# Loading x in quarters and beginning attention on the first of them

## The chip, the cores and the metric

One Trainium2 chip, one of its cores. The metric is the time of the kernel on the device in microseconds (us), the median of several runs. The core has a matrix engine (TensorE, PE), a vector engine (VectorE, DVE), an engine for activation functions (ScalarE, ACT), a general one (GpSimd, POOL), and a queue engine that issues most of the transfers (SyncE, SP). Each works through its own list of instructions in order and waits on semaphores for the others.

## The reference

Two attention blocks over sequences of 2048 rows with 1024 features, 32 heads of 32 features each. Their outputs stand side by side in the result. All tensors are bf16.

```python
def A(x, wqkv, wo):                       # plain softmax attention
    q, k, v = split(x @ wqkv)             # 32 heads, 2048 x 32 each
    p = softmax(q @ k.T * 32 ** -0.5)     # over all 2048 keys, no mask
    return concat_heads(p @ v) @ wo

def B(x, wq, wk, wv, wo, beta):           # four segments of 512 rows, one after the other
    for s in range(4):
        a_dot = softmax(q_s @ k_s.T * scale + causal_mask) @ v_s
        a_mem = phi(q_s) @ M / (phi(q_s) @ z + 1e-6)
        o_s = sigmoid(beta) * a_mem + (1 - sigmoid(beta)) * a_dot
        M += phi(k_s).T @ v_s ; z += sum(phi(k_s))
    return concat(o) @ wo
```

Block A dominates: 32 heads of 2048 x 2048 scores, every one of which goes through an exponential.

## The kernel before

**Tiling.** The 32 heads of A are worked in eight groups of four (`g`, 0 to 7). A group's queries are cut into eight chunks of 256 (`c`). Scores are computed transposed, keys on the 128 partitions: a tile is 512 columns, two blocks of 128 keys (`kt`) by 256 queries of one head. Two or three such tiles make one exponential on ACT (`plan_op`, line 774), 128 x 1536 or 128 x 1024, from PSUM to a tile `P` in SBUF. PSUM has eight banks: two slots of three banks take the scores in turn (`SLOT_BANKS`), bank 6 (`X_BANKS`) serves all projections one after the other, bank 7 collects the attention output. Lines 823 and 829 multiply `P` with the values and with ones, for the output and for the softmax's denominator; `norm` divides (lines 847 to 898).

**Guard.** The exponential needs an upper bound of the scores as its bias, or it could overflow. It comes from the squared lengths of keys and queries: squares (`square_dve` or `square`), a product with `blk32` that sums them by head (`guard_cols`, line 989), a maximum over columns (line 996), a spreading of the results over partitions by a product with ones (`guard_end`, line 1016 and a product at line 450), another maximum (line 1026), and the bias column (line 1034).

**Order.** The work is listed with keys (`item`), and a scheduler in the Python program (`Prog.schedule`) lays it out once, by planned costs and due times, into one fixed list per engine. Exponentials follow the order of `units`; the projections of later groups, B's work and the output projections are `jobs` with an earliest and a latest time, spread by `level` and placed between score tiles by `pick`. The constants `STICK`, `OVER`, `MARGIN`, `LEAD_A`, `DUE_SLOPE`, `XR`, `OUT_D` steer that placement. What the program writes down is only the order; the engines then run as their semaphores allow.

**Beginning** (`plan_prologue`). ACT issues the loads of group 0's key and query weights (`W_A`). SP issues x of A, transposed on the way: eight transfers of 1024 rows x 128 features for the first half, then the value weights `Wv_A`, then eight for the second half (line 1052). PE multiplies the first half (`half0`): keys and queries 0 to 1023 of group 0, in banks 0 to 3. Then the first guard, in bias column 16 (`BIAS0`), and the value products (`job_VA`), of which three are evicted by ACT (line 1142).

**First half of the keys.** All of group 0's first four chunks run over the first half of the keys only (`part` 0: tiles 0 to 3), with that guard; their unnormalized results are parked in `OT_B`, which is still free (line 878). When the second half of keys and queries has been projected, the guard is renewed over all keys (`guard_A0`); the parked results are scaled by `f0`, the exponential of the difference of the two biases (line 1004), and added to the second half's (`part` 1, line 881). B's x (`xT_B`, line 950), its weights and beta (`graw`, line 1089) are loaded by SP behind A's x.

Of the kernel before, what the change touches and what calls it, by code (L numbers as in the profile page):

```python
# [5 lines left out]
dt = mybir.dt  # L6
# [4 lines left out]
P = 128  # L11
# [19 lines left out]
BIAS0 = 16  # L31
# [14 lines left out]
class Group:  # L46

    __slots__ = ("pe", "rd", "left", "free")

    def __init__(self):  # L50
        self.pe, self.rd = [], []
        self.left, self.free = 0, 0.0
# [82 lines left out]
STICK = 0  # L135
OVER = 0.1
# [3 lines left out]
MARGIN = 1.5  # L140
FILL = 0.0
RXJ = 4
LEAD_A, LEAD_B, DUE_AT, DUE_SLOPE = 12.0, 12.0, 8.0, 0.5
HOLD = {}
XR = 6
XC = 0
OUT_D = 60.0
# [3 lines left out]
class Prog:  # L151
# [39 lines left out]
    def schedule(self):  # L191
        pend = {}
        groups = list(dict.fromkeys(o.grp for o in self.ops if o.grp is not None))
        for g in groups:
            own = {*g.pe, *g.rd}
            first = g.pe[0]
            first.gate = [(x, 0.0) for o in g.pe[1:] for x in (o.deps | o.order) - own]
            first.gate += [(x, sum(o.dur for o in g.pe)) for o in g.rd for x in (o.deps | o.order) - own]
            g.left = len(g.rd)
            assert g.rd and not any(x.grp is g and x not in own for x in first.deps)  # L200
# [48 lines left out]
        def pick(t, av, c):  # L249
# [8 lines left out]
            best = None  # L258
            for x in av:
                if x.urgent:  # L260
                    continue
                if x.pvn is None and x.key > st["prog"] + AHEAD and not cold:
                    d = x.dur + (SWITCH if x.mode != mode else 0.0)
                    if x.key < st["prog"] + FILL and d <= slack + OVER:
                        v = (False, 1e3, x.key)
                        if best is None or v < best[0]:
                            best = (v, x)
                    continue
                d = x.dur + (SWITCH if x.mode != mode else 0.0)
# [9 lines left out]
                v = (d > slack + OVER, k, x.key)  # L279
# [138 lines left out]
class _Kernel:  # L418
# [74 lines left out]
    def alloc(self):  # L493
# [6 lines left out]
        self.r_xT = [[Res(), Res()] for _ in range(8)]  # L500
# [70 lines left out]
        self.f0 = sb("f0", [P, 1], dt.float32)  # L571
        self.r_f0 = Res()
# [5 lines left out]
        self.sm_xT = [[self.sem(f"d_xT{i}{h}") for h in range(2)] for i in range(8)]  # L578
# [13 lines left out]
    def plan(self):  # L592
# [14 lines left out]
        units = [("A", 0, c, p) for p in range(2) for c in range(4)] + [u + (None,) for u in units[4:]]  # L607
        tiles = [self.tiles_att_A(i, k, p) if kind == "A" else self.tiles_att_B(i, k) for kind, i, k, p in units]
        n = 0
        while n < len(units):  # L610
# [4 lines left out]
            if n == 0:  # L615
# [6 lines left out]
    def joins(self, a, b):  # L622

        return a[0] == b[0] == "A" and a[1] == b[1] and (a[3] == 0) == (b[3] == 0)
# [36 lines left out]
    def tiles_att_A(self, g, c, part=None):  # L661
# [3 lines left out]
        lo, hi = (0, 8) if part is None else (4 * part, 4 * part + 4)  # L665
        for t in range(lo, hi):
# [3 lines left out]
            for h in range(4):  # L670
                tiles.append(dict(unit=("A", g, c), kind="A", g=g, c=c, h=h, w=512, pieces=pieces, set=key, part=part, pv=pv,
                                  bias=BIAS0 if part == 0 else g % 2))
# [192 lines left out]
    def norm(self, t, key):  # L865
# [6 lines left out]
        if t["part"] is not None:  # L872
# [3 lines left out]
            if t["part"] == 0:  # L876
# [4 lines left out]
            self.dve(lambda e: e.scalar_tensor_tensor(out=st1, in0=st1, scalar=self.f0[:, 0:1], in1=src, op0=ALU.mult,  # L881
                                                      op1=ALU.add), 512, k, [ob, self.r_f0] + rs1, rs1)
# [3 lines left out]
        if kind == "A":  # L886
            T2, r2 = self.recip_rows(lsrc, ro, QC, k)
            q = QC * t["c"]
            if g >= 6 and self.r_xT[g][0].tag == ("dead",):
                rd = self.r_OTx[g - 6][t["c"]] = Res()  # L890
                self.pg.after(rd, self.r_xT[g][t["c"] // 4])
# [70 lines left out]
    def xbank(self):  # L962
        b = X_BANKS[0]
        self.bank[b] = Res(Group())
# [17 lines left out]
    def guard_cols(self, key, sqs, ncols):  # L982

        b = self.xbank()
# [15 lines left out]
    def guard_A0(self, key):  # L1000
        col = self.guard_cols(key, self.sqA[(0, 0)] + self.sqA[(0, 1)], 512)
        self.guard_end(key + 0.2, [self.col0, col], 2, [0], halves=True)
        rb, r0 = self.r_bias[0], self.r_bias[BIAS0]
        x = self.act(lambda e: e.activation(self.f0[:, :], self.bias[:, BIAS0:BIAS0 + 1], ACT.Exp, bias=self.bias[:, 0:1],
                                            scale=-1.0), 1, key + 1.0, [rb, r0], [self.r_f0])
# [5 lines left out]
    def guard_end(self, key, cols, nper, bias_cols, halves=False):  # L1011
# [6 lines left out]
        b = self.xbank()  # L1018
# [481 lines left out]
```

## Time and profile before

| | |
|---|---|
| three runs | 1207.85 us median, 1207.67 to 1208.72 |
| the profiled execution | 1211.64 us |
| its span, first to last instruction | 1209.8 us |
| ACT / PE / DVE / POOL busy | 1167.5 / 1128.0 / 557.7 / 216.6 us |
| DMA | 65.68 MB moved, 54 GB/s over the span |
| mean granted PE clock | 0.990 |

The profile is one execution on the chip. Its page gives busy time by engine, groups of instructions by line of the program with the mean duration of one (ns) and the idle time ahead of them with what ended it, and the chain of work that ended last. The trace behind it can be asked for a timeline of one engine (start, duration, engine, line, operation, tiles), for the rows of one tile, and for busy times in chosen stretches. In a timeline, `x15` means that 15 instructions of a kind followed one another and the duration covers all of them. Letters after an engine, as in SPq and ACTq, are its queue: the issuing of a transfer, which counts as time of the issuing engine and is not the transfer itself.

### The profile page before, as it was taken

What the parts mean: (1) busy time and instruction counts of PE and PEld (TensorE: products, weight loads), DVE (VectorE), ACT (ScalarE), POOL (GpSimd) and SP (SyncE); (2) the same over time, 40 slices, a digit from 0 to 9 for tenths busy, and PEclk for the clock granted to TensorE, in tenths of its full rate; (3) what the DMA queues carried; (4) which work ended last, traced back from release to release, by engine and by line L of the source; (5) the groups of instructions that cost most, each with busy time, mean ns of one, the idle gap of its engine ahead of it and who ended that gap; (6) DMA issues with size and microseconds to landing.
All of it is one profiled execution on the core that took longest, in us unless ns stands there. A gap on an engine that the chain in (4) does not pass through costs nothing.

```text
span 1209.8 us, 52848 instructions
## 1 busy us (share of the span) xinstructions
PE 1128.0 (93%) x24712; PEld 544.6 (45%) x24712; DVE 557.7 (46%) x1254; ACT 1167.5 (96%) x867; POOL 216.6 (18%) x279
## 2 busy tenths in 40 slices
PE   6999999999999999989999999999899999989997
PEld 4444434464444445534444444454444444433443
DVE  1243353443443545556453564565435555543224
ACT  3899999999999999999999999999999999998997
POOL 1121131311320211122210330312103221010000
PEclk9999999999999999999999999999999999998999
DMA  9812323202111312202301122102112410000101
GB/s 176 207 37 53 85 53 57 63 16 68 52 30 46 72 41 42 65 22 51 85 18 42 41 51 50 54 22 46 53 51 59 147 26 12 29 20 28 37 29 36
DMA packets 165675, 65.68 MB, mean 54 GB/s; under 512 B 135248, under 2 KB 162640, under 8 KB 165456
## 3 DMA queue, kind: packets, MB, share of 16 engines
q1 hardware_dynamic: 163088, 61.51, 20.8%
q8 instruction: 193, 3.16, 1.1%
q10 hardware_dynamic: 2368, 0.79, 0.3%
q14 instruction: 26, 0.21, 0.1%
HBM read 39.00 MB, written 11.73 MB: 42 GB/s over the span
## 4 chain that ended last, share of the span: by engine, by line
ACT 69%; PE 21%; DVE 5%; issue 3%; SPq 1%; DMA 1%; POOL 0%; DVEq 0%; ACTq 0%
ACT P L774 67%; PE ps L450 11%; PE ps L759 5%; PE ps L823 3%; PE ps L829 2%; ACT PKQ_B L1174 1%; SPq L1052 1%; DVE T L847 1%; DVE PKQ_B L1179 1%; DMA Wv_A<-in_A_wqkv_dram 1%; DVE KQ_B L973 0%; DVE T L856 0%; POOL P L786 0%; DVE OT_B L1200 0%; DVE KQ_A L973 0%
## 5 line engine op out<-in xcount | busy, mean ns | idle before, releaser
L774 ACT ACTIVATE P<-ps,bias 128x1536 bf16<-128x1536 f32 (+3 forms) x826 | 1149.1, 1664 | 16.2 <-PE ps L759 8.0
L829 PE MATMUL ps<-P,onesb 128*32 128x256 bf16 (+1 forms) x4864 | 300.1, 271 | 0.0
L759 PE MATMUL ps<-KQ_A 32*128 32x256 bf16 x4096 | 277.1, 275 | 19.3 <-ACT P L774 15.8
L823 PE MATMUL ps<-P,V_A 128*32 128x256 bf16 x4096 | 259.3, 276 | 8.5 <-ACT P L774 7.0
L759 PEld LDWEIGHTS ps<-KQ_A 32*128 32x128 bf16 x4096 | 80.6, 92 | 240.6 <-ACT P L774 130.7
L450 PE MATMUL ps<-xT_A,W_A 128*32 128x512 bf16 x2048 | 147.5, 390 | 11.4 <-DMA xT_A<-in_A_x_dram 6.5
L450 PE MATMUL ps<-xT_B,W_B 128*32 128x512 bf16 x2048 | 142.0, 381 | 4.4 <-DVE cols L996 1.4
L823 PEld LDWEIGHTS ps<-P,V_A 128*32 128x32 bf16 x4096 | 108.8, 96 | 79.0 <-issue 41.8
L829 PEld LDWEIGHTS ps<-P,onesb 128*32 128x32 bf16 x4864 | 130.7, 97 | 26.2
L786 POOL TENSOR_SCALAR_AFFINE_SELECT P<-P 128x768 bf16<-128x768 bf16 (+2 forms) x128 | 81.7, 662 | 254.9 <-ACT P L774 254.8
L979 POOL TENSOR_TENSOR sqB<-KQ_B 128x512 bf16<-128x512 bf16 x64 | 67.2, 1049 | 319.7 <-DVE KQ_B L973 274.9
L979 POOL TENSOR_TENSOR sqA<-KQ_A 128x512 bf16<-128x512 bf16 x60 | 63.1, 1051 | 293.5 <-DVE KQ_A L973 218.7
L973 DVE CAST KQ_B<-ps 128x512 bf16<-128x512 f32 x64 | 44.1, 690 | 123.6 <-PE ps L450 122.2
L1250 DVE CAST outsb<-ps 128x512 bf16<-128x512 f32 x56 | 38.7, 691 | 135.2 <-PE ps L450 134.1
L847 DVE STREAM_TRANSPOSE T<-ps 128x256 f32<-128x256 f32 (+1 forms) x148 | 72.5, 490 | 54.1 <-PE ps L829 39.8
L973 DVE CAST KQ_A<-ps 128x512 bf16<-128x512 f32 x60 | 41.5, 691 | 119.9 <-PE ps L450 116.1
L450 PE MATMUL ps<-Wv_A,xT_A 128*32 128x256 bf16 x2048 | 71.7, 274 | 6.6 <-issue 2.4
L856 DVE STREAM_TRANSPOSE T<-rc 128x256 f32<-128x256 f32 (+1 forms) x152 | 73.3, 485 | 4.0
L450 PEld LDWEIGHTS ps<-xT_A,W_A 128*32 128x32 bf16 x2048 | 45.7, 97 | 63.1 <-issue 31.7
L450 PE MATMUL ps<-Wv_B,xT_B 128*32 128x512 bf16 x1024 | 70.5, 382 | 2.4 <-DVE KQ_B L973 0.6
L450 PE MATMUL ps<-Wo_B,OT_B 128*32 128x512 bf16 x1024 | 70.8, 389 | 1.0 <-DVE KQ_B L973 0.6
L450 PEld LDWEIGHTS ps<-xT_B,W_B 128*32 128x32 bf16 x2048 | 45.6, 95 | 52.2 <-issue 25.5
(82 smaller groups left out, 754.4 us busy)
## 6 DMA issues: line engine op xcount, KB each, us to landing
Wv_B<-in_B_wv_dram SPq DMA_DIRECT2D x8, 1024.0 KB, 5.9
W_B<-in_B_wk_dram SPq DMA_DIRECT2D x32, 256.0 KB, 3.1
W_B<-in_B_wq_dram SPq DMA_DIRECT2D x32, 256.0 KB, 3.1
out_dram<-outsb SPq DMA_DIRECT2D x56, 128.0 KB, 1.9
W_A<-in_A_wqkv_dram SPq DMA_DIRECT2D x14, 256.0 KB, 3.2
ot_a_scratch<-OTst SPq DMA_DIRECT2D x51, 64.0 KB, 1.8
xT_A<-ot_a_scratch SPq DMA_DIRECT2D x6, 512.0 KB, 7.5
Wv_A<-in_A_wqkv_dram SPq DMA_DIRECT2D x4, 512.0 KB, 5.4
```

The costliest lines, as they stand in the source:

```text
L450: ins = e.matmul(out[r], w[:, r], x, start=start, stop=stop, tile_position=(0, 32 * t), skip_group_check=True)
L759: ins = e.matmul(out, kap, qap, start=st, stop=True, tile_position=(32 * h, 0), skip_group_check=True)
L774: a = self.act(lambda e: e.activation(dst, src, ACT.Exp, bias=self.bias[:, bc:bc + 1], scale=SCALE), cols, key, res + [self.r_bias[bc]], [rP])
L786: self.pool(lambda e, v=v, pat=pat: e.affine_select(v, v, pattern=pat, compare_op=ALU.is_ge, fill=0.0, base=0, channel_multiplier=-1), (m ...
L823: ins = e.matmul(self.ps[32 * h:32 * h + 32, 512 * obk + q0:512 * obk + q0 + nq], vt[:, c0 + 32 * h:c0 + 32 * h + 32], Pt[:, b, off:off + nq],
L829: ins = e.matmul(self.ps[32 * h:32 * h + 32, lcol + q0:lcol + q0 + nq], self.onesb[:, 0:32], Pt[:, b, off:off + nq], start=False, stop=las ...
L847: self.dve(lambda e: e.transpose(T1[:, 0:n], src), n, key, rsrc, [r1])
L856: self.dve(lambda e: e.transpose(T2[:, 0:n].rearrange("p (b r) -> p b r", r=32), bc), n, key, [rr], [r2])
L973: self.dve(lambda e: e.tensor_copy(dst, out), ncol, key + 1.0, [self.bank[b]], rdst)
L979: self.pool(lambda e: e.tensor_tensor(sq[:, :], src, src, ALU.mult), 512, key, [rsrc], [rs], rate=0.5)
L1052: self.dma(lambda e, i=i, h=h: e.dma_start(self.xT[:, i, 1024 * h:1024 * h + 1024], xa[1024 * h:1024 * h + 1024, P * i:P * i + P], transpo ...
L1250: self.dve(lambda e: e.tensor_copy(ob[:, :], self.ps[:, 512 * b:512 * b + 512]), 512, key + 1.0, [self.bank[b]], [ro])
```

## The change

x is loaded in quarters of 512 rows: 32 transposing transfers in place of 16, with `Wv_A` behind the first eight. `half0` becomes `quarter`, called for the first and the second quarter. Attention begins with chunks 0 and 1 over the first quarter of the keys (`part` 0, four exponentials of 1536 columns and two of 1024), goes on with chunks 0 and 1 over the second quarter and chunks 2 and 3 over the first half (`part` 1, sixteen exponentials), then with all over the second half (`part` 2). The guard is renewed twice: from bias column 17 to 16 after the second quarter, and from 16 to 0 after the fourth; the parked results are scaled by `fp[:, 0]` and `fp[:, 1]`. While x loads, PE multiplies zeros (`warm`, seven sets of four products of 512 columns). Of the value products only the first is evicted by ACT. Some planner constants have other values, and `pick` weighs the openings of bank 6 one at a time.

```diff
-BIAS0 = 16
+BIAS_PART = (17, 16)
+PARTS = ((0, 0), (0, 1), (1, 0), (1, 1), (1, 2), (1, 3), (2, 0), (2, 1), (2, 2), (2, 3))
+WARM = 7
...
-STICK = 0
-OVER = 0.1
+STICK = 0.5
+OVER = 0.3
...
-MARGIN = 1.5
-FILL = 0.0
+MARGIN = 0.5
...
-LEAD_A, LEAD_B, DUE_AT, DUE_SLOPE = 12.0, 12.0, 8.0, 0.5
+LEAD_A, LEAD_B, DUE_AT, DUE_SLOPE = 15.0, 12.0, 8.0, 0.3
-XR = 6
+XR = 0
-OUT_D = 60.0
+OUT_D = 90.0
...
-        units = [("A", 0, c, p) for p in range(2) for c in range(4)] + [u + (None,) for u in units[4:]]
+        units = [("A", 0, c, p) for p, c in PARTS] + [u + (None,) for u in units[4:]]
...
-        lo, hi = (0, 8) if part is None else (4 * part, 4 * part + 4)
+        lo, hi = {None: (0, 8), 0: (0, 2), 1: (2 if c < 2 else 0, 4), 2: (4, 8)}[part]
...
+    def guard_more(self, key, sqs, i, old, new):
+
+        ci, rc = self.guard_cols(key, sqs)
+        self.bank[X_BANKS[0]].grp.chain = True
+        c0, r0 = self.colrun
+        self.dve(lambda e: e.tensor_tensor(self.cols[:, ci:ci + 1], self.cols[:, ci:ci + 1], self.cols[:, c0:c0 + 1], ALU.max), 1,
+                 key + 0.1, [rc, r0], [rc])
+        self.colrun = (ci, rc)
+        self.guard_end(key + 0.2, [self.colrun], 2, [new], bank=X_BANKS[0])
+        x = self.act(lambda e: e.activation(self.fp[:, i:i + 1], self.bias[:, old:old + 1], ACT.Exp, bias=self.bias[:, new:new + 1],
+                                            scale=-1.0), 1, key + 1.0, [self.r_bias[old], self.r_bias[new]], [self.r_fp[i]])
+        x.margin = MARGIN
...
+        def warm(key):
+            self.dve(lambda e: e.memset(dummy[:, :], 0.0), 512, key, (), [rd])
+            for _ in range(WARM):
+                self.pe(lambda e: self.mm4(e, self.ps[:, 512 * 5:512 * 6], dummy[:, 0:P], dummy[:, :], True, True), 0.43, key, [rd],
+                        [self.bank[5]])
+        self.item(-99.5, warm)
...
-            for h in range(2):
+            for h in range(4):
                 for i in range(8):
                     mark([self.r_xT[i][h]], "x")
-                    self.dma(lambda e, i=i, h=h: e.dma_start(self.xT[:, i, 1024 * h:1024 * h + 1024],
-                                                             xa[1024 * h:1024 * h + 1024, P * i:P * i + P], transpose=True),
-                             self.sm_xT[i][h], key, [], [self.r_xT[i][h]], issue=1.55 + 0.1 * h, lat=3.2)
+                    self.dma(lambda e, i=i, h=h: e.dma_start(self.xT[:, i, 512 * h:512 * h + 512],
+                                                             xa[512 * h:512 * h + 512, P * i:P * i + P], transpose=True),
+                             self.sm_xT[i][h], key, [], [self.r_xT[i][h]], issue=0.68 if h < 2 else 0.85, lat=3.2)
...
+            if c == 0:
+                for x in self.r_KQA[0]:
+                    mark(x, "KQ", 0)
+                self.colrun = self.guard_cols(key, sq, bank=3)
+                self.guard_end(key, [self.colrun], 2, [BIAS_PART[0]], bank=4)
+            else:
+                self.guard_more(key, sq, 0, *BIAS_PART)
+        self.item(-50.0, lambda key: quarter(key, 0, (0, 1)))
+        self.item(-49.0, lambda key: self.job_VA(0, 0, key, 5, "ACT"))
+        self.item(-48.0, lambda key: quarter(key, 1, (6, 7)))
+        self.item(-47.0, lambda key: self.job_VA(0, 1, key, behind=True))
...
+        for c in (2, 3):
+            for kq in range(2):
+                add(8.0 * c - 9.0, p2 - 4.0, KQ, lambda key, kq=kq, c=c: self.job_KA(0, kq, c, key))
+        add(15.0, p2 - 4.0, 0.4, lambda key: self.guard_A0(key + 2.0))
```

## The prediction

> **What bounds the kernel now.** I read the page's busy shares first, then the ACT timeline for the gaps, then the beginning: SP's timeline, and the rows of the transposing loads by tile.
>
> ```profile
> PE 1128.0 (93%) x24712; PEld 544.6 (45%) x24712; DVE 557.7 (46%) x1254; ACT 1167.5 (96%) x867; POOL 216.6 (18%) x279
> L774 ACT ACTIVATE P<-ps,bias 128x1536 bf16<-128x1536 f32 (+3 forms) x826 | 1149.1, 1664 | 16.2 <-PE ps L759 8.0
> ```
>
> ScalarE (ACT) bounds it: 826 exponentials, 96% of the span. So the time is: start of the first exponential, plus the exponentials, plus ACT's gaps, plus the tail. The ACT timeline gives all four:
>
> ```profile
> 22.30 1.54 ACT L774 ACTIVATE P<-ps,bias 128x1536 bf16<-128x1536 f32 x1 [0.84 <-DVE bias L1034]
> 26.60 21.81 ACT L774 ACTIVATE P<-ps,bias 128x1536 bf16<-128x1536 f32 x15
> 50.23 5.41 ACT L774 ACTIVATE P<-ps,bias 128x1536 bf16<-128x1536 f32 x4 [1.82 <-PE ps L759]
> 58.41 2.97 ACT L774 ACTIVATE P<-ps,bias 128x1536 bf16<-128x1536 f32 x2 [1.48 <-DVE bias L1034]
> 64.87 101.94 ACT L774 ACTIVATE P<-ps,bias 128x1536 bf16<-128x1536 f32 x71
> 1166.39 35.63 ACT L774 ACTIVATE P<-ps,bias 128x1536 bf16<-128x1536 f32 x26 [1.05 <-PE ps L829]
> ```
>
> The first exponential (no. 1) starts at 22.30. A streaming one takes 21.81/15 = 1.454 us, one of 1024 columns about 1.05 (50.23 to 55.64 is three and one). No. 23, the first with the second guard, starts at 58.41, no. 26 at 64.87; from there gaps are rare. They add up to 3.8 us between 179 and 573 and 5.3 us between 1088 and 1167. The tail after 1202.0 is 7.8 us. The span is 1209.8; the profiled execution took 1211.64, which is 3.79 above the median 1207.85.
>
> What feeds no. 1 is A's x, loaded by SP:
>
> ```profile
> 0.81 11.72 SPq L1052 DMA_TRANSPOSE xT_A<-in_A_x_dram  x8
> 12.57 0.58 SPq L931 DMA_DIRECT2D Wv_A<-in_A_wqkv_dram  x1
> 200.61 11.66 SPq L950 DMA_TRANSPOSE xT_B<-in_B_x_dram  x8
> L1052 SPq DMA_TRANSPOSE xT_A<-in_A_x_dram x16: 1272/1301/3708, 0.8 to 26.5; - x16
> L950 SPq DMA_TRANSPOSE xT_B<-in_B_x_dram x32: 1122/1262/2310, 29.7 to 754.5; - x32
> L1215 SPq DMA_TRANSPOSE PKt_B<-PKQ_B x96: 1095/1234/2462, 175.3 to 851.4; - x96
> DMA to landing us min/median/max: 2.4/3.6/5.5
> ```
>
> (Minimum, median, maximum ns of one issue; the last line belongs to xT_B.) This decides the case. Issuing one transpose costs SP 1.30 us for 1024 rows, 1.26 for 512 and 1.23 for 128. The price is per issue, not per byte. Eight of 512 rows took 11.66 us at 200 us, where little else loads; eight of 1024 took 11.72. That is 1.46 each with the longer ones among them.
>
> **The change, part by part.**
>
> *Quarters.* 16 issues become 32. At 1.465 (11.72/8) the first quarter's last issue starts at 0.81 + 7 x 1.465 = 11.07 and lands 3.6 later, at 14.7; the half of before was in use at about 15.1, so 0.4 is won. Wv_A still lands at about 18.65 (issued at 12.57; PE's first product with it ran 6.1 later): its place behind eight issues is unchanged. The second quarter starts at 13.2 and its last piece lands at 13.2 + 7 x 1.465 + 3.6 = 27.05. Of the fourth, the last issue starts at 0.81 + 31 x 1.465 + 0.63 = 46.9 and lands at 50.5; before, SP had issued all of x at 28.45. The ends: 1.26 + 0.05 between issues, and 1.53, the mean of xT_B's 32 with the waits between them; the fourth quarter then lands at 45.7 or 52.5. I take 1.465, the price of the same eight places in the same queue.
>
> *The first exponential.* PE's new order is: dummies, first-quarter products with four of the second quarter among them, scores no. 1, the guard's column product, 52 value products (they need Wv_A), the guard's spreading product. Before, the same wait stood there. From the rows: 18.65 + 1.59 (52 value products) + 1.11 (spreading product at 21.19 to exponential at 22.30) = 21.35. The value eviction (0.60, ACT) ends near 21.5. So no. 1 starts at 21.5: 0.8 won. Two value evictions leave ACT, about 0.5 each, and one tiny exponential more comes in; both lie before no. 8 and are in the times below.
>
> *Dummy products.* 28 products, seven sets of four; the first real sets of before stand 0.43 us apart until 11.1 and about 0.21 later, so the dummies take 7 x 0.43 = 3.0 us, from about 1 to 4, ahead of the first x at 6.5. They cost nothing (3.0 if x were there at 1). They win nothing either, or at most 0.5: the products behind them wait for x.
>
> *Six exponentials, then a second guard.* PE's queue holds the scores of no. 2 behind the second quarter's fifth piece, no. 3 behind its seventh, no. 4 behind its eighth. Piece by piece (1.465 apart) that puts no. 2 at 23.2, no. 3 at 26.2, no. 4 at 27.05 + 0.3 + 0.35 = 27.7. Nos. 5 and 6 (1024 columns) follow at 29.1 and 30.3. The guard's renewal runs from 27.05: products 0.3, two casts 1.38, two squares 0.71, column product 0.45, reductions, spreading and bias 0.69 + 0.16 + 0.29 + 0.45 + 0.29 + 0.21, and about 0.2 of handing over: no. 7 starts at 32.2. Before had finished the same columns (4 + 2 x 1024/1536 = 5.33 long exponentials) at 26.60 + 3.33 x 1.454 = 31.4. The gain has turned into 0.8 lost.
>
> *Further DVE and PE work.* Two more merges of 0.69 on DVE (46% busy), one more guard on PE (0.9): counted in the guard's chain above, else hidden by idle DVE; bare, 2 us.
>
> *To the third guard.* Nos. 7 to 16 stream: 10 x 1.454 and 0.1, so no. 17 starts at 46.8. The scores of no. 18 stand in PE's queue behind the last piece of x: 50.5 + 0.1 + 0.35 = 51.0, a gap of 2.7. Behind it come 0.66 of attention products, a key/query job of 1.75 and more: no. 19 at 54.0, nos. 20 to 22 at 55.45, 56.9 and 58.35. The third guard's spreading product stands behind scores no. 24, which need no. 22 finished (59.8): 59.8 + 0.33 + 0.44 + 0.4 + 0.3 + 0.3 puts no. 23 at 61.6, and no. 26 at 66.0 against 64.87: 1.15 lost.
>
> *What slides behind x.* Before, PE stalled three times for nothing the profile shows between 48 and 62 us, while the loads of B's weights kept all DMA engines busy; ACT's gaps there are 1.82, 0.18 and 1.66, together 3.66. They are inside the 64.87. After, those loads are issued from 61.7, behind x (48.3), W_A (49.6) and eight transposes of B's x (61.3). The same stalls should fall after no. 23, with more slack on PE: by counts of instructions and rows, PE has 10.2 us of work for nos. 25 to 32, which take ACT 11.6. Between 0 and 3.66; I take 1.8. The loading of beta slides to 61.9 as well and took 6.9 to land: 68.8 + 0.75 of DVE copies = 69.6, where ACT wants it at the end of no. 27, 68.9. DVE's queue holds value casts behind those copies. 0.7; between 0 and 1.6.
>
> *The new planner constants.* They reorder PE's jobs over the whole run. ACT's list keeps all 826 exponentials in the same shapes. I counted PE's work per eight exponentials in both orders, with the rows' durations. At the end they agree: 4.9 and 5.1 us in the light stretch, then 10.7 and 10.7, 12.0 and 12.2. So the late loss stays:
>
> ```profile
> 1080.00:1090.00 10.00, 7.32 (x146) 2.93 (x134) 3.04 (x7) 9.72 (x9) 2.49 (x4) 0.82 0.05 15
> 1090.00:1100.00 10.00, 8.48 (x98) 2.34 (x92) 3.96 (x11) 9.63 (x7) 0.00 (x0) 0.50 0.01 2
> ```
>
> (PE, PEld, DVE, ACT, POOL busy, granted clock, DMA.) PE, with little to do, drops to clock 0.50, then has too much and ACT waits 5.3 us. Nothing in the new order fills that stretch. The middle counts as 0, between -3 (its 3.8 us of gaps gone) and +3.
>
> Sum: 1.15 + 1.8 + 0.7 = 3.65. From the profiled 1211.64 that is 1215.3, less 3.79 **1211.5 us**.
>
> **The rivals.**
>
> *Bytes set the price* (faster). If half the rows cost half, an issue is 0.65: the first quarter lands at 9.3, Wv_A about 12.4, no. 1 starts at 12.4 + 1.59 + 1.11 = 15.1. The second guard (17 + 5.1 = 22) is ready before the six exponentials end (23.0), and x never holds PE, which then is the bound: 26.0 us of work for nos. 9 to 24. No. 25 then falls near 54 to 57 against 63.23: 6 to 8 won, **1201**. Against it: 96 issues of 128 rows at 1.23. For it: planned costs in the code, 0.68 and 0.85. The Trainium skill, DMA: Bandwidth & Descriptors, "Latency and other measured facts", gives DMA transposes 261 GB/s; by that an estimate for a quarter of 1 MB is 4 us, and this rival would be right. The 128-row issues disagree with any rule by bytes. Chance 0.17.
>
> *Bare issues* (no change). Without the long ones an issue is 1.26 + 0.05. Then the fourth quarter lands at 45.7, no. 18 does not wait, no. 26 comes at about 61.1: 3.8 won, of which 2.3 goes back to the sliding stalls: **1206.3**. For it: five of the first eight in a row took 1.30. Against: every load of B's x has issues of 1.8 to 2.3 among its eight. Chance 0.20.
>
> *A light stretch in the middle* (slower still). The new order leaves PE 6.7 us of work for one run of eight exponentials (about nos. 441 to 448) and 11.3 for the next; before had no such pair there. Half the late loss, 2.7: **1214.2**. Against: stretches of 8.1 to 8.7 passed before. Chance 0.12.
>
> **How the numbers follow.** The forecast has 0.51. About 0.2% (2.4 us) is what a measurement of this kernel can tell from no change: 1205.4 to 1210.3 counts as the same. Faster: 0.17, 0.07 of the second rival, 0.02 of the forecast's lower end, 0.26. Same: 0.13 and 0.08, 0.21. Slower: 0.53. The range, 1203 to 1216, leaves out the first rival and a little above; the forecast's own range is 1208 to 1216.
>
> **What would show it.** Right: xT_A issues near 1.26 to 1.46 each, first exponential at 20 to 22, gaps before nos. 2, 3 and 18, no. 26 at 65 to 67. Wrong: issues near 0.7, a first exponential near 15, no gap at x's last piece, or ACT's later gaps adding up to far from 9 us.

## The result, and the profile after

The changed kernel takes 1229.53 us (median of 6 runs, 1225.24 to 1231.76) where the kernel before takes 1209.26 (6 runs): ratio 1.0163, 95% interval 1.0138 to 1.0187. It is slower by 1.6%, five times what was forecast (1211.5 against 1207.85 is 0.3%) and outside the range. The profiled execution took 1230.99 us, its span is 1229.3: 19.5 us over that of before.

Two lines of the page of the changed kernel, busy time and the group of exponentials:

```profile
PE 1140.8 (93%) x24752; PEld 549.6 (45%) x24752; DVE 566.2 (46%) x1264; ACT 1167.9 (95%) x865; POOL 217.8 (18%) x279
L774 ACT ACTIVATE P<-ps,bias 128x1536 bf16<-128x1536 f32 (+3 forms) x826 | 1148.6, 1573 | 22.0 <-PE ps L759 11.0
```

ACT works as long as before (1167.9 against 1167.5 us). What grew is its idle time, and the waits of ACT say for whom:

```profile
ACT P L774 <- PE ps L759: 11.0, 15, 2.6
ACT PKQ_B L1199 <- DMA PKt_B<-PKQ_B: 10.2, 4, 3.6
ACT P L774 <- PE ps L829: 9.5, 10, 2.0
```

(Who waited, for what: us in total, times, the longest.) The second row did not exist before: 10.2 us in which ACT waits for a transfer. L1199 writes phi(q) and phi(k) of B into `PKQ_B`, a ring of two; before it may overwrite a buffer, the eight transposes `PKt_B` must have read it. The ACT timeline places these waits and those of the start:

```profile
23.88 7.84 ACT L774 ACTIVATE P<-ps,bias 128x1536 bf16<-128x1536 f32 x6
32.15 1.54 ACT L774 ACTIVATE P<-ps,bias 128x1536 bf16<-128x1536 f32 x1 [0.44 <-DVE bias L1044]
...
38.12 1.54 ACT L774 ACTIVATE P<-ps,bias 128x1536 bf16<-128x1536 f32 x1 [1.38 <-PE ps L829]
41.29 8.70 ACT L774 ACTIVATE P<-ps,bias 128x1536 bf16<-128x1536 f32 x6 [1.63 <-PE ps L829]
51.29 8.69 ACT L774 ACTIVATE P<-ps,bias 128x1536 bf16<-128x1536 f32 x6 [1.30 <-PE ps L829]
61.96 1.54 ACT L774 ACTIVATE P<-ps,bias 128x1536 bf16<-128x1536 f32 x1 [1.98 <-PE ps L829]
...
72.29 5.83 ACT L774 ACTIVATE P<-ps,bias 128x1536 bf16<-128x1536 f32 x4 [1.36 <-PE ps L759]
80.73 1.54 ACT L774 ACTIVATE P<-ps,bias 128x1536 bf16<-128x1536 f32 x1 [2.60 <-PE ps L759]
83.45 7.49 ACT L774 ACTIVATE P<-ps,bias 128x1536 bf16<-128x1536 f32 x5 [1.18 <-PE ps L759]
...
227.24 0.63 ACT L1199 ACTIVATE PKQ_B<-KQ_B 128x512 bf16<-128x512 bf16 x1 [3.58 <-DMA PKt_B<-PKQ_B]
...
498.99 1.06 ACT L1199 ACTIVATE PKQ_B<-KQ_B 128x1024 bf16<-128x1024 bf16 x1 [3.51 <-DMA PKt_B<-PKQ_B]
...
749.65 1.06 ACT L1199 ACTIVATE PKQ_B<-KQ_B 128x1024 bf16<-128x1024 bf16 x1 [2.80 <-DMA PKt_B<-PKQ_B]
```

These start exponentials nos. 1, 7, 10, 11, 17, 23, 29, 33 and 34; the phi ones stand ahead of nos. 132, 323 and 496. A fourth, of 0.34 us, stands ahead of no. 532. The 19.5 us divide as follows. No. 34 starts at 83.45; before it started at 76.5, eight streaming exponentials behind no. 26: 7.0. ACT's gaps from there to no. 750 add up to 16.12 us where there were 3.76: 12.4, of which 10.2 is the wait for `PKt_B`. The gaps from no. 751 on fell from 5.3 to 3.2: -2.1. The remaining 2.2 are other work of ACT and gaps too short for the timeline.

SP's timeline, and the row of x's transposes by tile:

```profile
0.80 10.34 SPq L1071 DMA_TRANSPOSE xT_A<-in_A_x_dram  x8
11.19 0.58 SPq L934 DMA_DIRECT2D Wv_A<-in_A_wqkv_dram  x1
11.82 35.62 SPq L1071 DMA_TRANSPOSE xT_A<-in_A_x_dram  x24
...
68.05 2.80 SPq L1392 DMA_DIRECT2D Wo_B<-in_B_wo_dram  x1
...
214.57 11.54 SPq L1240 DMA_TRANSPOSE PKt_B<-PKQ_B  x8
```

```profile
L1071 SPq DMA_TRANSPOSE xT_A<-in_A_x_dram x32: 1224/1262/2522, 0.8 to 46.2; - x32
```

Half the rows cost nearly the same: 1.26 us in place of 1.30. x is issued until 47.4 us in place of 28.5, and the loads behind it move by 18 to 19 us: `Wo_B` from 50.2 to 68.1. And a set of eight `PKt_B` takes SP 11.54 us; the planner in the code counts 5.6 (`issue=0.7`).

Last, PE's timeline:

```profile
17.81 0.62 PE L450 MATMUL ps<-xT_A,W_A 128*32 128x512 bf16 x4 [4.26 <-DMA xT_A<-in_A_x_dram]
...
19.73 2.99 PE L450 MATMUL ps<-Wv_A,xT_A 128*32 128x256 bf16 x52
...
71.65 0.27 PE L829 MATMUL ps<-P,onesb 128*32 128x256 bf16 x1 [1.34 <-issue]
...
79.77 0.59 PE L450 MATMUL ps<-xT_A,W_A 128*32 128x512 bf16 x5 [2.72 <-issue]
```

The two stalls marked "issue" are of the kind that before fell between 48 and 62 us: PE waits for no semaphore, while the weights load (329 GB/s between 75 and 80 us). They are what ACT pays before nos. 29, 33 and 34.

The packets in the trace show what PE lacks. Its instructions come by DMA too, on a queue of their own (packets, MB, share of the 16 DMA engines):

```profile
q8 instruction: 194, 3.18, 1.1%
```

PE has 49,681 records in this trace (matmuls, weight loads and its sequencer's), so one packet of 16 KB stands for 256 of them. The two stalls lie at records 2497 and 2753, exactly 256 apart, and PE goes on 1.5 and 1.3 us after the end of such a packet. These two packets began 3.1 and 5.8 us after PE had entered the 256 records before, while 234 and 310 GB/s were moved; the next two began after 1.1 and 0.1 us, at 90 GB/s and less. In all traces of this document the 18 stalls of this kind between 40 and 85 us lie at such steps of 256 and end 1.3 to 1.5 us after a packet. So PE has run out of instructions there, and the next ones come late while the weights load.

### The profile page after: what moved, and what is told of

It reads as the page before. It is cut to its first block, busy times and chain, and to the rows that moved or that the text cites. A ratio compares the mean times of both kernels' runs of the same rounds, so it can differ in the third digit from the quotient of the medians.

```text
span 1229.3 us, 52960 instructions
## 1 busy us (share of the span) xinstructions
PE 1140.8 (93%) x24752; PEld 549.6 (45%) x24752; DVE 566.2 (46%) x1264; ACT 1167.9 (95%) x865; POOL 217.8 (18%) x279
## 4 chain that ended last, share of the span: by engine, by line
ACT 60%; PE 26%; DVE 5%; SPq 4%; issue 3%; DMA 1%; POOL 1%; ACTq 0%; DVEq 0%
ACT P L774 58%; PE ps L450 13%; PE ps L759 6%; PE ps L823 4%; PE ps L829 3%; SPq L1240 3%; ACT PKQ_B L1199 1%; DVE T L847 1%; DMA PKt_B<-PKQ_B 1%; SPq L1071 1%; DVE T L856 1%; POOL P L786 1%; DVE PKQ_B L1204 1%; DMA xT_A<-in_A_x_dram 0%; DVE KQ_A L979 0%
## 5 line engine op out<-in xcount | busy, mean ns | idle before, releaser
L829 PE MATMUL ps<-P,onesb 128*32 128x256 bf16 (+1 forms) x4864 | 301.5, 272 | 1.3 <-issue 1.3
L759 PEld LDWEIGHTS ps<-KQ_A 32*128 32x128 bf16 x4096 | 80.9, 93 | 241.0 <-issue 142.8
L829 PEld LDWEIGHTS ps<-P,onesb 128*32 128x32 bf16 x4864 | 131.5, 98 | 25.1 <-issue 1.3
```

The lines of the kernel that those rows point to most:

```text
L759: ins = e.matmul(out, kap, qap, start=st, stop=True, tile_position=(32 * h, 0), skip_group_check=True)
L829: ins = e.matmul(self.ps[32 * h:32 * h + 32, lcol + q0:lcol + q0 + nq], self.onesb[:, 0:32], Pt[:, b, off:off + nq], start=False, stop=las ...
```

## The experiments

The theory after the comparison had two causes: (a) the quarters push all later loads back into a stretch where PE cannot afford its stalls, 7 us; (b) the new order puts phi exponentials too close behind the transposes they must wait for, 10 us. Ratios are to the kernel before on the same chip. "In its exact order" means that the plan was made first and only the named transfers were changed afterwards.

| | edit | us | ratio, 95% interval |
|---|---|---|---|
| e1 | x in halves | 1221.72 | 1.0110, 1.0091 to 1.0128 |
| e2 | `Wo_B` later | 1226.96 | 1.0139, 1.0116 to 1.0162 |
| e3 | true price of phi's transposes | 1219.93 | 1.0092, 1.0077 to 1.0107 |
| e4 | longer phi ring | 1219.39 | 1.0092, 1.0075 to 1.0109 |
| e5 | before + new constants | 1232.54 | 1.0193, 1.0176 to 1.0209 |
| e6 | old constants | 1219.08 | 1.0080, 1.0067 to 1.0093 |
| e7 | e1 and e3 | 1214.66 | 1.0044, 1.0032 to 1.0057 |
| e8 | before, x in whole columns | 1218.19 | 1.0067, 1.0055 to 1.0079 |
| e9 | no dummies | 1227.81 | 1.0147, 1.0125 to 1.0168 |
| e10 | e7 and old constants | 1212.96 | 1.0020, 1.0007 to 1.0033 |
| e11 | e10 and `Wo_B` later | 1209.76 | 1.0005, 0.9994 to 1.0017 |
| e12 | before, `Wo_B` later | 1207.85 | 0.9982, 0.9970 to 0.9994 |

**e1: x in halves.** The transfers of the odd quarters are taken out after the plan is made, and who needed one waits for the even one, now of 1024 rows:

```diff
-                    self.dma(lambda e, i=i, h=h: e.dma_start(self.xT[:, i, 512 * h:512 * h + 512],
-                                                             xa[512 * h:512 * h + 512, P * i:P * i + P], transpose=True),
-                             self.sm_xT[i][h], key, [], [self.r_xT[i][h]], issue=0.68 if h < 2 else 0.85, lat=3.2)
+                    self.xops[i, h] = self.dma(lambda e, i=i, h=h: e.dma_start(
+                        self.xT[:, i, 512 * h:512 * h + 1024], xa[512 * h:512 * h + 1024, P * i:P * i + P], transpose=True),
+                        self.sm_xT[i][h], key, [], [self.r_xT[i][h]], issue=0.68 if h < 2 else 0.85, lat=3.2)
...
+        for (i, h), o in self.xops.items():
+            if h % 2:
+                first = self.xops[i, h - 1]
+                for x in self.pg.ops:
+                    if o in x.deps:
+                        x.deps.remove(o)
+                        x.deps.add(first)
+                self.pg.ops.remove(o)
+                self.pg.queue["SP"].remove(o)
```

> The changed kernel in its exact order on every engine, but x of A comes in 16 transposing loads of 1024 rows in place of 32 of 512; whoever needs a quarter waits for the half it lies in. SP has then issued x some 19 us earlier. Theory (two causes: the quarters push every later load back into a stretch where PE cannot afford its stalls, about 7 us; and waits of ScalarE for the transposes of phi(k), about 10 us): the first exponential is no earlier (22 to 24 us), the PE stalls without a cause move from 70 to 80 us back to 50 to 62 us, no. 34 starts at 78 to 80 in place of 83.45, and the three waits for phi(k) stay: 1225 us, ratio to before 1.012 to 1.014. Rival 1, the quarters are the whole loss (all that follows is shifted by them, the phi(k) waits too): ratio within 0.002 of 1.000. Rival 2, the attention on two chunks with its extra guards is what costs the start, whatever x's pieces are: no. 34 at 83 or later, ratio 1.016 or more, because the first exponentials now also wait for the half.

The ACT timeline of this kernel around the stretch in question:

```profile
60.28 1.54 ACT L786 ACTIVATE P<-ps,bias 128x1536 bf16<-128x1536 f32 x1 [1.98 <-PE ps L841]
61.72 0.28 ACT L1029 ACTIVATE fp<-bias 128x1 f32<-128x1 f32 x1
61.90 5.82 ACT L786 ACTIVATE P<-ps,bias 128x1536 bf16<-128x1536 f32 x4
67.59 0.23 ACT L1132 ACTIVATE gc<-gc 128x8 f32<-128x8 f32 x1
67.69 25.89 ACT L786 ACTIVATE P<-ps,bias 128x1536 bf16<-128x1536 f32 x18
```

No. 23 starts at 60.28, and from there no gap: no. 34 (the seventh of the last row) starts at 76.2, as in the kernel before (76.5). So the 7 us of the start are the quarters', all that this trace of the changed kernel shows; in the medians the halves win 0.0053, 6.4 us. More was won than the theory expected (78 to 80): PE's stalls were to move back to 50 to 62 us, and none came, though the same loads are issued from 43 to 57 us. The phi waits stay, 8.3 us. Rival 1 (the quarters are the whole loss) and rival 2 (the two chunks cost the start) both fall.

**e2: `Wo_B` later.** In SP's queue only:

```diff
+        q = self.pg.queue["SP"]
+        q.remove(self.op_wob)
+        n = next(n for n, o in enumerate(q) if o.sem is self.sm_PKt)
+        q.insert(n, self.op_wob)
```

> The changed kernel in its exact order on every engine, but in SP's queue the load of B's output weights (Wo_B) stands just ahead of the first transposes of phi(k), far from the loads of the other weights. Theory: the PE stalls that no wait explains (1.34 us at 70.3, 2.72 at 77.1) come while the weights load at 280 to 410 GB/s; with one large load fewer they shrink, ScalarE's gaps before nos. 29, 33 and 34 (5.1 us in sum) go by 2 to 4, and the time is 1226 us, ratio 1.013 to 1.015. Rival, the stalls belong to PE's own work there (the order of its jobs, its lowered clock of 0.59) and not to the loads: gaps of 5 us again, 1229.5 us, ratio 1.016. If the one load was all of it and the stalls come only from its collision with W_B and W_A: gaps under 0.5 and 1224.5.

The profile has one gap of 2.31 us before no. 26 where the changed kernel had 1.36, 2.60 and 1.18. But e9, with the load in its old place, has 1.6 us of gaps there, so one trace does not show what the move does. The time falls as expected, but the intervals of both overlap: alone, it is a hint. e11 and e12 make the same move in other orders.

**e3: the true price in the plan.**

```diff
-  self.sm_PKt, key, self.r_PKt, reads=rp, issue=0.7, lat=3.0
+  self.sm_PKt, key, self.r_PKt, reads=rp, issue=1.42, lat=2.7
-  self.sm_xTB, key, self.r_xTB, issue=0.8, lat=3.0
+  self.sm_xTB, key, self.r_xTB, issue=1.46, lat=3.6
```

> The changed kernel, but the planner that writes the order counts a transposing issue of phi(k) with 1.42 us and one of B's x with 1.46 (the trace's durations in queue) in place of 0.7 and 0.8. The order of all engines is planned anew with these. Theory: ScalarE's waits for the transposes of phi(k) (3.58 us before no. 132, 3.51 before no. 323, 2.80 before no. 496, 0.34 before no. 532) exist because the plan thinks the eight issues take 5.6 us where they take 10 to 11.5; with the true price the plan keeps the phi exponentials apart and the waits go: 10 us less, about 1219.5 us, ratio 1.007 to 1.010, with no. 34 still near 83. Rival 1, the phi(k) waits only stand where other waits would be anyway (the loss is in the order, PE or DVE becomes late next): ratio 1.014 to 1.017. Rival 2, a plan with other prices differs by chance anywhere: any ratio from 1.000 to 1.020 with gaps at new places.

Of its waits of ACT, the row in question:

```profile
ACT PKQ_B L1199 <- DMA PKt_B<-PKQ_B: 0.5, 1, 0.5
```

10.2 us have become 0.5. The ratio falls by 0.0071, 8.6 us. The theory's number was met, against rival 1. The new plan differs elsewhere too: no. 34 starts at 80.9 and not near 83, and there are other small gaps between nos. 408 and 481, 3.6 us, so rival 2 has a small share.

**e4: a longer ring.** The wait taken away by room, with the planner's wrong price left as it is:

```diff
-        self.PKQ = [sb(f"PKQ_B{i}", [P, 2, L]) for i in range(2)]
+        pkq = sb("PKQ_B", [P, 6, L])
+        self.PKQ = [pkq[:, j:5 + j % 2:4 - 2 * (j // 2), :] for j in range(4)]
```

`PKQ[j % 2]` becomes `PKQ[j % 4]` throughout; for the room, `outsb` has 3 buffers in place of 4, `OTst` 2 in place of 3, and `cols` and `bias` are shorter.

> The changed kernel, but the raw phi(q)/phi(k) tiles are four buffers (in part the same memory for the q halves) in place of two, so that the next phi exponentials need not wait for the transposes of the last phi(k); two small staging rings (outsb, OTst) give up one buffer each for the room. The order is planned anew. Theory: the 10.2 us of waits for the phi(k) transposes vanish because nothing is overwritten, and nothing else asks for them so soon: 1219.5 us, ratio 1.007 to 1.010. Rival 1: the transposes are needed by PE just as soon, so the wait moves from ScalarE's exponentials to PE's products and comes back as gaps of the same size: 1.015 to 1.017. Rival 2: the replanned order and the smaller staging rings bring losses of their own: over 1.017, with waits for outsb or OTst.

The row of `PKQ_B` is gone from ACT's waits, and the time is that of e3. So nobody else needed those transposes so soon: the wait was only that for the buffer. Two edits with nothing in common but this wait, and that the order was planned anew, win the same 0.7%.

**e5: the new constants alone.** The kernel before, with the seven constants that the diff changes:

```diff
-STICK = 0
-OVER = 0.1
+STICK = 0.5
+OVER = 0.3
...
-MARGIN = 1.5
+MARGIN = 0.5
...
-LEAD_A, LEAD_B, DUE_AT, DUE_SLOPE = 12.0, 12.0, 8.0, 0.5
+LEAD_A, LEAD_B, DUE_AT, DUE_SLOPE = 15.0, 12.0, 8.0, 0.3
...
-XR = 6
+XR = 0
...
-OUT_D = 60.0
+OUT_D = 90.0
```

> The kernel before with one part of the change alone: the planner's new constants (STICK, OVER, MARGIN, LEAD_A, DUE_SLOPE, XR, OUT_D). x in halves, attention beginning as before. Theory: it is these constants that put the phi exponentials so close behind the transposes of phi(k). In this plan the exponentials that overwrite PKQ stand, with 1.43 us an issue, 4.5 us too early after no. 133, 5.0 after no. 172, 3.4 after no. 321 and 4.7 after no. 531 (the kernel before: never too early). ScalarE then waits for PKt at these four places, 9 to 14 us in sum, and the start is as before (no. 34 within 1 us of 76.4): 1217 to 1223 us, ratio 1.007 to 1.012. Rival, the phi waits come with the earlier start of attention and not with the constants: no such wait, ratio within 0.003 of 1.000.

```profile
ACT PKQ_B L1174 <- DMA PKt_B<-PKQ_B: 17.2, 4, 9.3
```

Four waits, at the four places named, but 17.2 us and not 9 to 14, and so a ratio above the 1.007 to 1.012 expected: the one before no. 134 is 9.30. There the set is issued at 216.24, behind five transposes of `xT_B` and a load, and takes 12.85. No. 34 starts at 78.1, 1.7 us late and not within 1. Constants that look like tuning of PE's order cost 1.9% by themselves, as much as the whole change (the intervals overlap), and x still comes in halves. The rival falls.

**e6: the changed kernel with the old constants.** The diff of e5 the other way round, in the changed kernel:

```diff
-STICK = 0.5
-OVER = 0.3
+STICK = 0
+OVER = 0.1
...
```

> The changed kernel with the constants of before: quarters, dummies, attention on two chunks and the extra guards, but planned with the old STICK, OVER, MARGIN, LEAD_A, DUE_SLOPE, XR and OUT_D. Theory: one phi exponential (after no. 387) stands 3.1 us too early in this plan, the others 3.8 us or more late, so one wait of 2 to 3.5 us is left of the four; the loss of the start by the quarters stays, 5 to 9 us at no. 34. 1217 to 1221 us, ratio 1.007 to 1.011. Rival 1, the waits belong to the start: four of them, ratio 1.016. Rival 2, the start loses through the constants, not through the quarters: no. 34 at 78 or earlier, ratio 1.002 to 1.005.

One wait of 2.40 us for `PKt_B` is left, before no. 388, as the plan had it. No. 33 starts at 78.73 behind a gap of 2.68 and no. 34 at 80.3: a loss of the start is still there, though 3.8 us is less than the 5 to 9 expected. Rival 1 falls by the one wait, rival 2 by the ratio. The constants account for 0.8 of the 1.6%, by this order as by the price.

**e7: halves and the true price together.** The plan of e3, kept, and then the transfers of e1.

> Both mends together: the changed kernel planned with 1.42 and 1.46 us for the transposing issues of phi(k) and of B's x, that order kept, and then A's x in 16 issues of 1024 rows. Theory: the two causes are separate and add. From 1.0163 the halves took 0.0053 and the price 0.0071: 1.0039, 1213.2 us; no wait for PKt over 1 us, no. 34 within 1 us of 76.4. Rival, one and the same cause seen twice (phi waits shrink because everything behind x is earlier): about 1.009, as either alone. If the two chunks and the extra guards cost time of their own, more than the gap of 0.004 is left: 1.006 or more with ScalarE's gaps before nos. 7, 10, 11, 17 and 23.

1.0044 where the sum of the single gains gave 1.0039, and no. 34 at 76.5: the causes are separate and add. The rival (1.009) is outside the interval.

**e8: x in whole columns.** This asks after the price itself, in the kernel before in its exact order; the transfers of the second half are taken out as in e1, so there are 8 issues in place of 16:

```diff
-                    self.dma(lambda e, i=i, h=h: e.dma_start(self.xT[:, i, 1024 * h:1024 * h + 1024],
-                                                             xa[1024 * h:1024 * h + 1024, P * i:P * i + P], transpose=True),
+                    self.xops[i, h] = self.dma(lambda e, i=i, h=h: e.dma_start(
+                        self.xT[:, i, :], xa[:, P * i:P * i + P], transpose=True),
```

> The kernel before in its exact order, but A's x in 8 transposing issues of all 2048 rows in place of 16 of 1024. This asks what sets the price, at the other end of the quarters. Theory, a price per issue (1.23 us at 128 rows, 1.26 at 512, 1.30 at 1024): 1.35 to 1.6 us each, all of x there at some 15 to 17 us in place of 28.5 and more, the loads behind x some 11 us earlier, no. 2 no longer waiting for the second half (2.76 us won at most): 1205 to 1208 us, ratio 0.997 to 1.000. Rival, from 1024 rows on the bytes set the price (the row of 1024 is the highest of the three, and 2 MB in 11.7 us is 180 GB/s): 2.3 to 2.6 us each, no. 1 then waits for all of x and starts at about 30 in place of 22.3, and 1212 to 1217 us, ratio 1.003 to 1.007.

SP's timeline, and the row by tile:

```profile
0.80 19.82 SPq L1065 DMA_TRANSPOSE xT_A<-in_A_x_dram  x8
```

```profile
L1065 SPq DMA_TRANSPOSE xT_A<-in_A_x_dram x8: 1398/2332/4397, 0.8 to 18.1; - x8
```

The theory fell, and the rival held: 2.33 us the median issue, 2.48 with the waits, no. 1 at 31.68, 0.7% slower. From 128 to 1024 rows the price is nearly flat (1.23 to 1.30; the 128-row pieces are read from SBUF, the others from DRAM); at 2048 it is 1.8 times as much. Where between 1024 and 2048 the bend lies was not measured. (The Trainium skill, DMA: Bandwidth & Descriptors, "Latency and other measured facts", gives DMA transposes 261 GB/s, measured on one kernel. Eight issues carry 1.05, 2.10 and 4.19 MB here in 10.34, 11.72 and 19.82 us: 101, 179 and 212 GB/s. The rate rises with the size of a piece and stays below that figure.)

**e9: no dummies.** All else stands in the same order:

```diff
-WARM = 7
+WARM = 0
```

> The changed kernel without its 28 dummy products (WARM = 0); every other instruction stands in the same order. Theory: they lie in time in which PE has nothing to do, and what PE lacks later is x: in the trace of the changed kernel its granted clock was 1.00 in the first 10 us, with the dummies, and 0.79 from 10 to 20, where it waits piece by piece. So they neither cost nor win: the first exponential within 1 us of the others' (20.4 to 23.9 us in the four orders with quarters or halves), 1228 to 1230.5 us, ratio 1.015 to 1.018. Rival 1, the dummies spend allowance and the lowered clock after 10 us is theirs: without them 1.00 in that stretch, no. 1 1 to 2 us earlier, ratio 1.0145 or less. Rival 2, they keep PE quick: without them the first products take longer and no. 1 comes 1 to 3 us later, ratio 1.018 or more.

The ratio is not to be told from that of the changed kernel. The stretches of its trace (PE, PEld, DVE, ACT, POOL busy, granted clock, DMA share, GB/s):

```profile
10.00:20.00 10.00, 6.40 (x86) 2.44 (x82) 2.43 (x5) 0.60 (x1) 0.00 (x0) 0.75 0.80 145
```

The clock falls without the dummies as well: 0.75, against 0.79 with them. Neither what the dummies were feared nor what they could be hoped to do is seen. The median, 1227.81, is 0.2 below what was expected, and the ratio lies between the theory's 1.015 and rival 1's 1.0145: an effect of 0.1 or 0.2% is not excluded.

The trace shows something else: the engines have the order of the changed kernel but for the dummies, and still ACT's one long gap between nos. 28 and 34 is this:

```profile
78.58 14.42 ACT L774 ACTIVATE P<-ps,bias 128x1536 bf16<-128x1536 f32 x10 [1.27 <-PE ps L759]
```

With 0.28 before no. 28 that is 1.6 us where the changed kernel's trace has 5.1. The loss behind x differs that much from one execution to another, unless the 28 dummies, which shift PE's steps of 256 records, are the reason.

**e10, e11: all mended, and `Wo_B` later as well.** e10 is e7 with the old constants; e11 makes in it the move of e2.

> All that was found, mended together: the changed kernel planned with the old constants and with 1.42 and 1.46 us for the transposing issues of phi(k) and B's x, and A's x in 16 issues of 1024 rows. Left of the change are the dummies, attention on two chunks over the first keys, and the extra guards. Theory: no wait for PKt (the nearest phi exponential stands 3.6 us behind its transposes in this plan), the start as in the kernel before at no. 26 (within 1 us of 64.9, because PE has the same products to do by then, with gaps before nos. 7, 10, 11, 17 and 23 in place of the one long one): from 1.0080 (old constants) less 0.0053 (halves) less 0.002 (the one wait left): 1.0007, between 0.999 and 1.003, 1208.5 to 1213 us. If attention on two chunks wins what it could (no. 1 at 20.4 in place of 22.3, no guard's wait of 1.5): ratio under 0.998. If it costs PE and DVE more than counted: 1.004 or more.

> The mended kernel, and in SP's queue the load of B's output weights just ahead of the first transposes of phi(k) as well; every other instruction in the same order. Theory: one large load fewer while PE is short of slack (48 to 62 us); of ScalarE's gaps there 1 to 2.5 us go, and the ratio is 0.001 to 0.002 under that of the mended kernel: 0.998 to 1.001. Rival: the load only moves its burst to 165 us, where it collides with the first transposes of phi(k), and PE and ScalarE stall there: no gain, or 0.001 worse.

With everything mended the attention on two chunks stands at 1.0020: no. 1 starts at 20.9 in place of 22.30, no. 23 at 60.9 in place of 58.41, no. 34 at 76.9. The earlier start is given back before no. 23, to gaps of 0.9 to 2.2 us that wait for PE, the one before no. 7 for the guard's bias. e11 brings 0.0015 more, to a ratio that cannot be told from 1. The size is as expected, the place is not: ACT's gaps between 48 and 62 us are the same in both (1.31 and 1.71), and neither has a stall of PE without a semaphore there. No. 34 starts 0.6 earlier, and the gaps from there to no. 750 are 3.8 in place of 5.6; why is open.

**e12: the kernel before, `Wo_B` later.** The move of e2 alone.

> The kernel before in its exact order, with only the load of B's output weights moved in SP's queue to just ahead of the first transposes of phi(k). Theory: ScalarE's gaps of 1.82, 0.18 and 1.66 us between 48 and 62 us come from PE's stalls while the weights load at 300 GB/s; with 2 MB less in that stretch 1 to 2.5 us of these go: 1206.5 to 1208.5 us against 1209, ratio 0.998 to 0.9993. Rival: the stalls are PE's own (weights of another kind of product) and stay, ratio 1.000, or the load disturbs the transposes at 165 us instead, ratio 1.001.

```profile
51.27 5.41 ACT L781 ACTIVATE P<-ps,bias 128x1536 bf16<-128x1536 f32 x4 [1.36 <-PE ps L766]
57.13 1.11 ACT L781 ACTIVATE P<-ps,bias 128x1024 bf16<-128x1024 f32 x1 [0.46 <-PE ps L766]
59.79 2.97 ACT L781 ACTIVATE P<-ps,bias 128x1536 bf16<-128x1536 f32 x2 [1.54 <-PE ps L450]
```

0.9982 (0.9970 to 0.9994): faster than the kernel before, by 0.2%. Of before's gaps in this stretch (1.82, 0.18, 1.48, 1.66) the last is gone and 1.36, 0.46 and 1.54 are left: 1.8 us won. One load of 2 MB that PE first uses at 364 us was standing among loads that were needed. PE's own stalls fit: 0.80, 0.49 and 1.95 us before, 0.40 and 0.76 here. The third is gone: the packet for which PE had waited there began 1.1 us after PE had entered the 256 records before, while 8 GB/s were moved, in place of 4.4 us and 356 GB/s. Loads alone do not make a stall: e1, e8 and e10 have `Wo_B` among the weights and no such stall between 40 and 85 us.

## Why the prediction was wrong, step by step

**Right: the price per issue.** It gave the issues of x 1.26 to 1.46 us; 1.26 was measured. All of x was to be issued at 48.3, and was at 47.4. Against the rival by bytes this was the decisive reading, and it held for the sizes in question; at 2048 rows (e8) the price is no longer one per issue.

**Right by luck: nos. 7, 23 and 26.** No. 7 came at 32.15 for 32.2, but not on the path that was forecast. x was to hold it, with gaps before nos. 2 and 3 and the second quarter's last piece at 27.05; that piece landed at 24.56, nos. 1 to 6 ran without a gap, and PE came late to the rest of that quarter's products (at 23.16), behind slow value products. No. 23 came at 61.96 for 61.6 and no. 26 at 66.4 for 66.0. Nos. 7 to 16 were to stream and no. 18 to wait 2.7 us for x's last piece. ACT waits instead before nos. 10, 11 and 17, 4.3 us, for PE's row sums (L829), and no. 18 not at all. e1 has the same gaps (2.19, 1.63, 1.31) with x there 19 us earlier: this part is bound by PE's jobs, not by x. The two errors cancel.

**Off: the first exponential.** 21.5 was forecast, 23.88 came. The step let the 52 value products begin when `Wv_A` lands, at 18.65, and took 1.59 us for them from the kernel before, where PE had its full clock. Here PE had stood idle for 4.26 us waiting for a piece of the second quarter; the products began at 19.73, the granted clock was 0.59 between 15 and 20 us, and they took 2.99. In e2, e3, e4, e6 and e9, with the same beginning, no. 1 started between 21.4 and 22.7.

**Mis-sized: "What slides behind x".** The mechanism was right and so was its place; the size was taken as 1.8 between 0 and 3.66, on the ground that PE had 10.2 us of work for 11.6 of ACT's. Measured: 1.36 + 2.60 + 1.18 = 5.1, with a slower clock that follows (0.66 between 80 and 85 us), which was left out. Together with no. 26 (1.6) this makes nearly all of the 7.0 us at no. 34; the sum had 3.65 by then. The size differs between traces: the six with quarters have 1.6 to 5.1 us there, the four with halves in the changed order (e1, e7, e10, e11) 0, 1.3, 0 and 0. So 1.8 lies within what single traces show; in the medians the quarters cost 6.4 us (e1) and 5.8 (e7 against e3), and the sum's 3.65 was too small. PE's slack, 11.6 less 10.2 us, could not hold a wait for its own instructions of up to 2.72. The term for beta (0.7) was 0.

**Failed: "The new planner constants … The middle counts as 0, between -3 … and +3".** This is the step that decides: 12.4 us there, 10.2 of them in a wait that the text does not mention. Only PE's work was counted in the two orders, because ACT's list "keeps all 826 exponentials in the same shapes". But ACT's list also holds the phi exponentials, and these moved towards the transposes ahead of them. All that was needed was on the table: the row of 96 issues at 1.23 us, shown as evidence for the price of x, against `issue=0.7` in the same planner. Worked out for each set, 8 x 1.43 + 2.7 us from its planned first issue to the planned phi exponential that overwrites its buffer: in the order before, the least slack is +0.1 us; in the changed order it is -4.6 (after no. 131), -2.1 (213), -2.7 (322), -4.3 (495) and -1.9 (531). ACT waited at four of these five, 3.58, 3.51, 2.80 and 0.34; in e9, with the same order, at all five (1.22 before no. 214). The kernel before was within its margin by chance: its planner had the same wrong price.

**The end.** "The late loss stays": it was 3.2 us, not 5.3. The rival of a light stretch at nos. 441 to 448 found nothing there. The prediction's sign of being wrong, later gaps far from 9 us, was plain: 19.3.

## What to carry to other kernels

When an order made by a planner is made anew, compare not only the bottleneck's work but every wait that the planner believes hidden: take each planned distance between a transfer and who needs its buffer, and set against it the duration from the trace. A wrong price in a planner costs nothing until some other constant uses up the slack that hid it. And where transfers are priced by the issue, cutting them for an earlier start moves everything behind them; ask first what the loads at the end of that queue will collide with, the engines' own instructions among it.

## What the runs showed of the hardware

- The median price of a transposing issue is nearly flat to 1024 rows of 128 features (1.23, 1.26 and 1.30 us at 128, 512 and 1024, the first read from SBUF) and is 1.8 times that at 2048 (2.33).
- PE's instructions arrive in packets of 16 KB, one for 256 of its records (194 packets, 49,681 records). In 18 stalls without a semaphore between 40 and 85 us, over all traces and all within a record of such a step of 256, PE went on 1.3 to 1.5 us after the end of a packet. In the changed kernel the two late packets began 3.1 and 5.8 us after PE had entered the 256 records before, while weights loaded at 234 and 310 GB/s.
- PE's granted clock falls to 0.5 to 0.6 in the 5 us that hold or follow a wait of 2.8 to 4.3 us for x (0.59 in the changed kernel, 0.51 in e9), and the same products then take 1.9 times as long. The Trainium skill, TensorE: Matmul & The Clock Gate, "Part 1: The HAM clock gate (the "warmup" mystery)", tells of half speed after an idle window of about 3.4 us that runs freely, so that the place shifts from run to run. The traces agree that it shifts: e11 has 0.50 between 10 and 15 us where e10 with the same beginning has 1.00, and e12 has 0.70 between 15 and 20 us with the same beginning that ran at 1.00 before, and there no. 1 came 1.4 us later. The wait of 2.8 us in e9 is shorter than that window.
